# Order and size of the first weight transfers in a fused attention and SwiGLU layer

## The chip, the cores and the metric

The kernel runs on one core of one Trainium2 chip. The metric is device microseconds from launch to end, the median of several runs. A profiled execution is one more run, with its own time; its span is the time from its first to its last instruction.

## The reference

For x of 2048 rows (S) and 576 columns (D), bfloat16, with 32 heads of 18 columns, a window of 256 rows and F = 4608:

```python
xn = layernorm(x)
q, k, v = heads(xn @ wqkv)                      # 576 x 1728
scores  = q @ k.T * 18 ** -0.5                  # masked to 0 <= i - j < 256
attn    = softmax(scores) @ v @ wo
h       = silu(xn @ w1) * (xn @ w3)             # gate and up, 576 x 4608
out     = x + attn + h @ w2                     # 4608 x 576
```

## The kernel before, in words

**Engines and terms.** TensorE multiplies (PE in the profile), VectorE (DVE) and ScalarE (ACT) evacuate PSUM and do elementwise work, GpSimd (POOL) copies and masks, SyncE (SP) does nothing but issue DMA transfers. Every operation is recorded with `add(engine, function, r=reads, w=writes, j=joins)`. A key such as `"wv"` names a buffer; a reader waits for all writers of its keys, and an operation with `j` is one more writer of the same contents. `dma=` names the semaphore of a transfer. Each engine then executes its own operations strictly in the order in which they were recorded, so an instruction that waits holds up all that stands behind it on its engine.

**Tiling.** Rows come in four chunks of 512 (`NC`, `CH`), each of four tiles of 128 (`TB`). The 576 columns over which most products sum are held as five blocks, four of 128 and one of 64 that lies on both halves of the partitions. Matmuls with a contraction of 64 run in pairs, one on each half of the array.

**The start (from L730 on).**
1. The x tiles are loaded on SP's and ScalarE's queues. SP then loads V's weights: blocks 0 to 3 in one transfer (L733, key `wv`); block 4 comes on ScalarE's queue (key `wvd`).
2. SP loads q and k's weights into `wa`, a scratch area within the buffer `pt`: the first column half of q and of k (L753, key `wqk0`), the last 64 rows of all columns on both partition halves (L757, key `wqkd`), then the second column half (L753, key `wqk1`).
3. For each x tile: layer norm on VectorE and GpSimd, transposition on TensorE (`xn_turn`, L374), evacuation by ScalarE into `xnT` (L381). In between, the V projections of the first two tiles run on TensorE. At the second tile (`i == 1`) SP is given the six transfers of the first gate/up weight set (`load_w13`, L315), which wait for that tile's evacuation. A set holds 512 columns of w3 on partitions 0 to 63 and of w1 on partitions 64 to 127, in nine row blocks of 64.
4. `xn_swap` (L394): two transfers on SP copy `xnT` to `xnS` with the partition halves exchanged, since each gate/up product needs its input on both halves. They wait for all four tiles.
5. GpSimd deals q and k's weights from `wa` to `wp` in the order of heads that the attention wants (L807): four copies for the first half (key `wp0`), three for the second (`wp1`). The clearing of buffers and the masks stand behind them on GpSimd.
6. TensorE runs V for tiles 2 and 3 and the projections `("q", 0)` to `("q", 3)` and `("8", 7)` (L429). A projection has two parts, of five and four row blocks; the first part of the next stands between them. The pairs of output tiles are (0, 1), (2, 3), (8, 4), (5, 6) and 7; tiles over 3 need `wp1` as well. After `("q", 0)` SP gets four transfers of gate/up set 1 and the spreading of k's rows for the first two groups; after `("q", 2)` the rest of these, and set 1's last two transfers.

**The units.** A chunk then has 36 units (`unit_pairs`, L660) of nine matmul pairs: one for each 128 columns of gate and up, the first four pairs from `xnT`, the next four from `xnS`, the last from `xnT`. Units 0 to 3 use gate/up set 0, units 4 to 7 set 1. Between the pairs the planner places the attention's steps: scores (L553), their exponentials (L562) and masks (L589). It counts the pairs in `clock`, starts at `start` (28 in chunk 0, 42 in the others), and spreads the 32 steps of chunk 0 evenly over what is left, at least 7.5 apart. The value products (L610) follow 20 counts after a pair of groups is complete. Last come the products with w2 and wo (L711, L717).

Of the kernel before, what the change touches and what calls it, by code (L numbers as in the profile page):

```python
# [44 lines left out]
class _Prog:  # L45
# [13 lines left out]
    def add(self, eng, fn, r=(), w=(), j=(), dma=None, after=()):  # L59
        deps = []  # L60
        for k in r:
            deps += self.bufs[k].writers
        for k in w:
            g = self.bufs.get(k)
            if g is not None:
                deps += g.ahead(eng)
        for k in j:
            g = self.bufs[k].before
            if g is not None:
                deps += g.ahead(eng)  # L70
        op = _Op(eng, fn, deps + list(after), dma)
        op.after = tuple(after)
        self.n[eng] += 1
        op.pos = self.n[eng]
        if dma is not None:
            self.dma_count[dma] = self.dma_count.get(dma, 0) + 16
            op.cnt = self.dma_count[dma]
        for k in r:
            self.bufs[k].readers.append(op)
        for k in w:  # L80
            self.bufs[k] = _Gen([op], self.bufs.get(k))
        for k in j:
            self.bufs[k].writers.append(op)
        for k in w:
            if self.bufs[k].before is not None:
                self.bufs[k].before.before = None
        self.ops.append(op)
        return op
# [76 lines left out]
def bass_parallel_sum__sliding_block__glu_gated_swiglu__prompt_kernel(  # L165
# [11 lines left out]
    D = A_x.shape[2]  # L177
# [18 lines left out]
    add = P.add  # L196

    with ExitStack() as es:
# [14 lines left out]
        xnT = sb("xnT", [128, 2, 5, CH])  # L213
        xnS = sb("xnS", [128, 4, CH])
        wv = sb("wv", [128, 5, D])
        wp = sb("wp", [128, 5, 9, 128])
        wo = sb("wo", [128, 5, D])
        w13 = [sb(f"w13_{i}", [128, 9, 512]) for i in range(NW13)]
# [75 lines left out]
        nfill = 0  # L294

        def w13_at(k):
            if k == 3:
                return NW13, hT[:, 18:27, :]
            s = (k if k < 3 else k - 1) % NW13
            return s, w13[s]  # L300
# [3 lines left out]
        def load_part(after=(), behind=()):  # L304

            nonlocal nfill
            if nfill >= 6 * NC * NFC:
# [9 lines left out]
                src[192 * part:192 * part + 192, c0:c0 + 512].rearrange("(kd p) f -> p kd f", p=64)),  # L317
                r=list(behind), after=after, dma=f"w13_{s}_{n}", **{"j" if i else "w": [("w13", s)]})

        def load_w13(behind=(), parts=6):  # L320
            for _ in range(parts):
                load_part((), behind)
# [68 lines left out]
        def xn_swap(c, eng):  # L391
            for n in range(2):
                p, q = 64 * n, 64 - 64 * n
                add(eng[n], lambda e, p=p, q=q: e.dma_start(  # L394
                    xnS[p:p + 64, :, :], xnT[q:q + 64, c % 2, 0:4, :]),
                    r=xk(c), dma=f"xnS{n}", **{"j" if n else "w": ["xnS"]})

        def xk(c):
            return [("xnT", c % 2, tt) for tt in range(TB)]
# [6 lines left out]
        def proj_part(c, what, banks, part, behind=()):  # L406

            kind, i = what
            last = []
            for n in range(5 - part):  # L410
                for r in range(2):
                    x = r ^ part
                    kd, r0 = (4 if n == 4 else n), 64 * r
                    rows = slice(r0, r0 + 64)
                    out_ = PS[:, banks[x], :]
                    if kind == "q":
                        t = pair_of(c, i)[x]
                        st, mv = wp[rows, kd, t, :], xnT[rows, c % 2, kd, :]
                        keys = ["wp0"] + (["wp1"] if t > 3 else []) + xk(c)
                    elif kind == "8":  # L420
                        out_ = PS[:, banks[x], 0:CH // 2]
                        st, mv = wp[rows, kd, i, :], xnT[rows, c % 2, kd, x * (CH // 2):(x + 1) * (CH // 2)]
                        keys = ["wp0", "wp1"] + xk(c)
                    else:
                        out_ = PS[:, banks[x], 0:HD]
                        st, mv = xnT[rows, c % 2, kd, i * 128:(i + 1) * 128], wv[rows, kd, x * HD:(x + 1) * HD]
                        keys = ["wvd" if n == 4 else "wv", ("xnT", c % 2, i)]
                    first = part == 0 and n == 0
                    op = add("pe", lambda e, out_=out_, st=st, mv=mv, n=n, r0=r0, first=first: e.matmul(  # L429
                        out_, st, mv, start=first, stop=(part == 1 and n == 3), tile_position=(r0, 0)),  # L430
                        r=keys, after=behind if n == 0 else (), **{"w" if first else "j": [("ps", banks[x])]})
                    if n == 4:
                        last.append(op)
            return last
# [216 lines left out]
        def unit_pairs(c, u, n0, n1, b0):  # L651

            fc, fl = divmod(u, 4)
            sl, wt = w13_at(c * NFC + fc)
            for n in range(n0, n1):
                for r in range(2):
                    r0 = 64 * r
                    k = 8 if n == 8 else (2 * n + r if n < 4 else 2 * (n - 4) + 1 - r)
                    src = xnT[r0:r0 + 64, c % 2, k // 2, :] if n in (0, 1, 2, 3, 8) else xnS[r0:r0 + 64, n - 4, :]
                    op = add("pe", lambda e, n=n, r0=r0, r=r, k=k, src=src: e.matmul(  # L660
                        PS[:, b0 + r, :], wt[r0:r0 + 64, k, fl * 128:(fl + 1) * 128], src,
                        start=(n == 0), stop=(n == 8), tile_position=(r0, 0)),
                        r=[("w13", sl), "xnS"] + xk(c), **{"j" if n else "w": [("ps", b0 + r)]})
            return op

        def unit_tanh(u, b0):
# [63 lines left out]
        xslot = {}  # L730
        for t in range(TB):
            xslot[t] = load_x(t, "act" if t % 2 else "sp")
        add("sp", lambda e: e.dma_start(  # L733
            wv[:, 0:4, :], A_wqkv[0:512, 2 * D:3 * D].rearrange("(kd p) f -> p kd f", p=128)),
            w=["wv"], dma="wv")
        for p in range(2):
            add("act", lambda e, p=p: e.dma_start(
                wv[64 * p:64 * p + 64, 4, p * HD:(p + 1) * HD], A_wqkv[512:576, 2 * D + p * HD:2 * D + (p + 1) * HD]),
                dma="wvd", **{"j" if p else "w": ["wvd"]})
# [10 lines left out]
        for h in range(2):  # L750
            for n in range(2):
                c0 = n * D + h * HD
                add("sp", lambda e, c0=c0: e.dma_start(  # L753
                    wa[:, 0:4, c0:c0 + HD], A_wqkv[0:512, c0:c0 + HD].rearrange("(kd p) f -> p kd f", p=128)),
                    dma=f"wqk{h}", **{"j" if n else "w": [f"wqk{h}"]})
# [15 lines left out]
        moves = [], []  # L771
        for i in range(TB):
            if i + 1 < TB:
                for p in range(2):
                    ln_stats(i + 1, xslot[i + 1], p)
            ln_apply(i, xslot[i])
            if i == TB - 1:
                for move in moves[1]:
                    move()
            xn_turn(i, JOBS[1] if i % 2 else SC, "act")  # L780
            if i == 0:
                warm(3, 3)
            if i == 1:
                load_w13([("xnT", 0, 1)])
            proj_end(moves)
            if i < TB - 2:
                proj_begin(0, ("v", i))
        xn_swap(0, ("sp", "sp"))
        for move in moves[0]:
            move()  # L790
        for tt in (TB - 2, TB - 1):
# [3 lines left out]
        dealt = []  # L795
        for h in range(2):
            a, b = 4 * h, 4 * h + 4
            moves = [(wpf[:, :, a:b, 0:2 * Dh], wf[:, :, 0, a:b, :]),
                     (wpf[:, :, a:b, 2 * Dh:7 * Dh // 2], wf[:, :, 1, a:b, 0:3 * Dh // 2])]
            lo, hi = ((0, SPREAD), (SPREAD + 1, G))[h]  # L800
            s0 = lo - h
            moves.append((wpf[:, :, 8, s0 * Dh // 2:(s0 + hi - lo) * Dh // 2].rearrange("p k (g c) -> p k g c", c=Dh // 2),
                          wf[:, :, 1, lo:hi, 3 * Dh // 2:2 * Dh]))
            if h == 0:
                moves.append((wpf[:, :, :, 63], wf[:, :, 1, SPREAD, 3 * Dh // 2:2 * Dh]))
            for n, (dst, src) in enumerate(moves):
                dealt.append(add("pool", lambda e, dst=dst, src=src: e.tensor_copy(dst, src),  # L807
                                 r=[f"wqk{h}", "wqkd"], **{"j" if n else "w": [f"wp{h}"]}))
        for n in range(6):
            P.bufs[("pt", n)] = _Gen([], None)  # L810
            P.bufs[("pt", n)].readers = list(dealt)
# [10 lines left out]
        for what in [("q", 0), ("q", 1), ("q", 2), ("q", 3), ("8", 7), None]:  # L822
# [9 lines left out]
            if got and got[0] == "q" and got[1] < 3:  # L832
                for buf, key, rows in (((wo, "woz", (64, 4, 5)), (oT, "oTz", (64, 4, 5))),
                                       ((wo, "woz", (96, 0, 4)),), ((oT, "oTz", (96, 0, 4)),))[got[1]]:
                    r0, k0, k1 = rows
# [7 lines left out]
        for c in range(NC):  # L843
# [6 lines left out]
            total = 9 * NF + len(att) + 3 * PV_COST  # L850
            if c:
                total += 9 * sum(COST[kind] for kind, _ in PROJ)
            start = 28 if c == 0 else 42
            last = total - 24
            nxt = soon = start
            clock = 0.0
# [55 lines left out]
            for u in range(NF):  # L912
# [6 lines left out]
                b0 = jobs[u] = job()  # L919
# [11 lines left out]
                if next_pv in pv_ready and clock >= pv_ready[next_pv] and next_pv < 3:  # L931
                    j = next_pv
# [15 lines left out]
                if u in stat:  # L948
                    t = (c + 1) * TB + stat[u]
# [4 lines left out]
                if u in apply:  # L954
                    t = (c + 1) * TB + apply[u]
# [5 lines left out]
                if c == 0 and u == 13:  # L961
                    for t in range(4):
                        rows = A_wo[252 * (t // 2):252 * (t // 2) + 252, :].rearrange("(s p d) f -> p s d f", p=2, d=Dh)[t % 2, :, :, :]
                        add("sp", lambda e, t=t, rows=rows: e.dma_start(wo[0:126, t, :], rows),
                            r=["woz"], dma="wo", **{"j" if t else "w": ["wo"]})
# [14 lines left out]
            for n, item in enumerate(p2_list(c)):  # L980
# [20 lines left out]
                elif n in (100, 120) and c + 2 < NC:  # L1001
                    t = (c + 2) * TB + (n == 120)
# [32 lines left out]
```

## Time and profile before

| what | us |
|---|---|
| median of 3 runs | 563.96 |
| lowest and highest of these | 563.29, 564.82 |
| profiled execution | 562.66 |
| its span | 560.9 |
| TensorE busy in the span | 555.9 (99%) |
| first matmul with a q/k weight | 13.89 after the start |
| first gate/up matmul | 23.14 after the start |

The span is 1.76 us shorter than the profiled execution's own time; that rest lies before the first and after the last instruction. The granted clock of TensorE is 1.00 throughout.

In what follows, a timeline line gives the start and length in us, the engine and line, the operation, what it writes and reads, the count, and in brackets how long the engine was idle before it and what released it. A line of the windows gives a stretch of time, its length, then the busy time of TensorE, its weight loads, VectorE, ScalarE and GpSimd with the instruction counts, the granted clock, the share of time in which the DMA engines were busy, and GB/s. A line of waits gives who waited for whom, the total in us, how many times, and the longest.

### The profile page before, as it was taken

The numbers are of one execution on the slowest core, as the hardware profiler recorded it, in microseconds if no ns is written. First come the engines' busy times: TensorE is split into PE (matmuls) and PEld (weight loads), VectorE is DVE, ScalarE is ACT, GpSimd is POOL, SyncE is SP. The second block draws the span as 40 slices with busy tenths as digits, with TensorE's granted clock in tenths as the row PEclk, the third lists the DMA queues.
The fourth block names the chain that finished last, engine by engine and source line by source line (L and its number), as shares of the span: only waits on it lengthen the run. The fifth ranks groups of instructions, "written<-read, shape, count | busy, mean of one in ns | idle before, by whom it ended". The sixth has DMA issues, their size and how long they took to land.

```text
span 560.9 us, 15712 instructions
## 1 busy us (share of the span) xinstructions
PE 555.9 (99%) x6767; PEld 330.6 (59%) x6767; DVE 314.1 (56%) x586; ACT 254.8 (45%) x349; POOL 163.4 (29%) x384
## 2 busy tenths in 40 slices
PE   8999999999999999999999999999999999999998
PEld 4445554677655455477765555547776455455776
DVE  7567798710356778851046678884114577777211
ACT  4366666100287776600038777650005767765000
POOL 5533444300033445330003345423000343432000
DMA  9996969996466459578646644956862675351552
GB/s 227 236 174 157 205 161 187 169 237 186 127 137 139 113 138 168 132 154 234 181 101 139 158 123 108 183 154 151 209 180 68 138 171 133 91 142 54 138 148 64
DMA packets 126562, 85.75 MB, mean 153 GB/s; under 512 B 33973, under 2 KB 124269, under 8 KB 126493
## 3 DMA queue, kind: packets, MB, share of 16 engines
q1 hardware_dynamic: 124629, 82.69, 63.8%
q10 hardware_dynamic: 1864, 2.07, 1.3%
q8 instruction: 53, 0.87, 0.7%
q14 instruction: 16, 0.13, 0.1%
HBM read 71.22 MB, written 2.36 MB: 131 GB/s over the span
## 4 chain that ended last, share of the span: by engine, by line
PE 97%; DMA 1%; SPq 1%; POOL 0%; issue 0%; DVE 0%; POOLq 0%
PE ps L660 50%; PE ps L711 25%; PE ps L429 9%; PE ps L553 6%; PE ps L610 4%; PE ps L717 3%; DMA pt<-in_A_wqkv_dram 1%; POOL wp L807 0%; SPq L753 0%; SPq L291 0%; SPq L757 0%; DVE ofin L724 0%; SPq L733 0%; POOLq L154 0%
## 5 line engine op out<-in xcount | busy, mean ns | idle before, releaser
L660 PE MATMUL ps<-xnT,w 64*128 64x512 bf16 x1400 | 181.9, 376 | 0.0
L660 PE MATMUL ps<-xnS,w 64*128 64x512 bf16 x1120 | 149.7, 376 | 0.0
L711 PE MATMUL ps<-w,hT 128*128 128x288 bf16 x1152 | 146.4, 286 | 0.0
L675 DVE SCALAR_TENSOR_TENSOR gs<-th,ps 128x512 bf16<-128x512 bf16 x144 | 98.0, 681 | 79.5 <-ACT th L669 78.8
L562 ACT ACTIVATE pt<-ps 128x1024 bf16<-128x1024 f32 (+1 forms) x112 | 113.2, 1010 | 60.0 <-PE ps L553 59.7
L711 PEld LDWEIGHTS ps<-w,hT 128*128 128x128 bf16 x1152 | 112.3, 98 | 28.9 <-issue 0.2
L589 POOL TENSOR_TENSOR pt<-pt,mk 128x128 int32<-128x128 int32 (+1 forms) x199 | 80.7, 426 | 88.5 <-ACT pt L562 88.5
L678 DVE SCALAR_TENSOR_TENSOR hT<-gs,ps 128x512 bf16<-128x512 bf16 x144 | 98.9, 687 | 5.0
L660 PEld LDWEIGHTS ps<-xnT,w 64*128 64x128 bf16 x1400 | 65.1, 94 | 61.4 <-DVE hT L678 0.2
L669 ACT ACTIVATE th<-ps 128x512 bf16<-128x512 f32 x144 | 85.5, 593 | 31.3 <-PE ps L660 30.8
L660 PEld LDWEIGHTS ps<-xnS,w 64*128 64x128 bf16 x1120 | 53.3, 94 | 57.0
L724 DVE TENSOR_TENSOR ofin<-ps,xp 128x288 bf16<-128x288 f32 x32 | 14.7, 458 | 124.4 <-PE ps L717 124.4
L442 ACT ACTIVATE stage<-ps 128x512 bf16<-128x512 f32 x16 | 9.5, 596 | 143.3 <-PE ps L429 141.0
L589 POOL TENSOR_TENSOR hT<-hT,mk 128x128 int32<-128x128 int32 (+1 forms) x31 | 12.4, 421 | 161.8 <-ACT hT L562 161.8
L553 PE MATMUL ps<-qv,kv 64*128 64x320 bf16 (+4 forms) x528 | 51.3, 260 | 0.0
L553 PEld LDWEIGHTS ps<-qv,kv 64*128 64x128 bf16 x528 | 25.0, 94 | 28.3 <-ACT hT L562 1.9
L429 PE MATMUL ps<-xnT,wp 64*128 64x512 bf16 (+1 forms) x360 | 37.8, 355 | 0.5 <-POOL wp L807 0.5
L632 DVE STREAM_TRANSPOSE od<-oq 128x256 bf16<-128x256 bf16 x64 | 25.8, 427 | 6.3 <-POOL oq L625 6.3
L562 ACT ACTIVATE stage<-ps 128x1024 bf16<-128x1024 f32 x24 | 24.6, 1024 | 10.2 <-PE ps L553 10.0
L429 PEld LDWEIGHTS ps<-xnT,wp 64*128 64x128 bf16 x360 | 17.4, 94 | 16.9 <-POOL wp L807 0.8
L717 PE MATMUL ps<-wo,oT 128*128 128x288 bf16 x160 | 24.8, 286 | 0.0
L429 PE MATMUL ps<-wv,xnT 64*128 64x288 bf16 x288 | 22.2, 283 | 0.6 <-DMA wv<-in_A_wqkv_dram 0.3
(58 smaller groups left out, 332.6 us busy)
## 6 DMA issues: line engine op xcount, KB each, us to landing
w<-in_B_w_dram SPq DMA_DIRECT2D x210, 192.0 KB, 4.2
w<-in_B_w_dram SPq DMA_DIRECT2D x72, 288.0 KB, 3.5
xp<-in_A_x_dram SPq DMA_DIRECT2D x28, 144.0 KB, 4.1
out_dram<-ofin SPq DMA_DIRECT2D x32, 72.0 KB, 3.2
xnS<-xnT SPq DMA_DIRECT2D x8, 256.0 KB, 4.8
oT<-od SPq DMA_DIRECT2D x48, 36.0 KB
pt<-in_A_wqkv_dram SPq DMA_DIRECT2D x4, 288.0 KB, 7.5
hT<-in_B_w_dram SPq DMA_DIRECT2D x6, 192.0 KB, 3.9
```

The costliest lines, as they stand in the source:

```text
L429: op = add("pe", lambda e, out_=out_, st=st, mv=mv, n=n, r0=r0, first=first: e.matmul(out_, st, mv, start=first, stop=(part == 1 and n == ...
L553: add("pe", lambda e, r0=r0, out_=out_, kb=kb, q0=q0, nb=nb: e.matmul(out_, kb4[r0:r0 + 64, g, kb + NV - NB, :] if kb < 0 else kv[r0:r0 + ...
L562: add("act", lambda e: e.activation(pt_slot(sl)[:, 0:w, :], PS[:, SC[0]:SC[1] + 1, 0:w].rearrange("p r q -> p q r"), ACT.Exp, scale=scale) ...
L589: add("pool", lambda e, vb=vb, mm=mm: e.tensor_tensor(vb, vb, mm, ALU.mult), r=(key if n == 0 else []) + ["mk"], **{"w" if n == 0 else "j" ...
L610: add("pe", lambda e, p=p, q=q, pr=pr, sl=sl, g=g, pos=pos, q0=q0, nb=nb, col=col, first=first, n=n: e.matmul(PS[32 * q:32 * q + VW, banks ...
L632: add("dve", lambda e: e.transpose(od[i][:, g % 2, c0:c0 + CH // 2], oq[:, c0:c0 + CH // 2]), r=["oq", "oq0"], **{"j" if half or g % 2 els ...
L660: op = add("pe", lambda e, n=n, r0=r0, r=r, k=k, src=src: e.matmul(PS[:, b0 + r, :], wt[r0:r0 + 64, k, fl * 128:(fl + 1) * 128], src, star ...
L669: add("act", lambda e: e.activation(th[i][:], PS[:, bg, :], ACT.Tanh, scale=0.5), r=[("ps", bg)], w=[("th", i)])
L675: add("dve", lambda e: e.scalar_tensor_tensor(out=gs[i][:], in0=th[i][:], scalar=1.0, in1=PS[:, bg, :], op0=ALU.add, op1=ALU.mult), r=[("t ...
L678: add("dve", lambda e: e.scalar_tensor_tensor(out=hT[:, u, :], in0=gs[i][:], scalar=0.5, in1=PS[:, bu, :], op0=ALU.mult, op1=ALU.mult), r= ...
L711: add("pe", lambda e: e.matmul(bank, hT[:, f, tt * 128:(tt + 1) * 128], w2[sl][:, k, :], start=(f == 0), stop=False), r=[("h", f), ("w2", ...
L717: add("pe", lambda e: e.matmul(bank, oT[:, k, tt * 128:(tt + 1) * 128], wo[:, k, d0:d0 + HD], start=False, stop=(k == 4)), r=[("oT", j) fo ...
```

## The change

- V's weights, blocks 0 to 3, come in two transfers of two blocks each (keys `wv0`, `wv1`). Each pair of V's matmuls waits for the transfer that holds its block.
- The first half of q and k's weights is dealt in eight copies in place of four: four for blocks 0 to 3, which wait for `wqk0` alone and write `wp0`, then four for block 4, which wait for `wqkd` and write a new key `wpr`. Only matmuls with block 4 (and those of tile 7, all of them) read `wpr`.
- Gate/up set 0 comes in two column halves of 256, each of two transfers with all nine row blocks. The first half (key `w13_first`) takes the place of the six transfers; the swap of the input follows it; then comes the second half. Units 0 and 1 of chunk 0 wait for the first half, units 2 and 3 for the second.
- The planner's `start` for chunk 0 goes from 28 to 32.

```diff
+        def load_first(half, behind=()):
+            nonlocal nfill
+            nfill = 6
+            s, dst = w13_at(0)
+            c0 = 256 * half
+            for n in range(2):
+                src = (B_w3, B_w1)[n]
+                add("sp", lambda e, n=n, src=src: e.dma_start(
+                    dst[64 * n:64 * n + 64, :, c0:c0 + 256],
+                    src[:, c0:c0 + 256].rearrange("(kd p) f -> p kd f", p=64)),
+                    r=list(behind), dma=f"w13_{s}_{n}" if half else f"w13_first_{n}",
+                    **{"j" if n else "w": [("w13", s) if half else "w13_first"]})
...
-                        keys = ["wp0"] + (["wp1"] if t > 3 else []) + xk(c)
+                        keys = ["wpr" if n == 4 else "wp0"] + (["wp1"] if t > 3 else []) + xk(c)
...
-                        keys = ["wp0", "wp1"] + xk(c)
+                        keys = ["wpr", "wp0", "wp1"] + xk(c)
...
-                        keys = ["wvd" if n == 4 else "wv", ("xnT", c % 2, i)]
+                        keys = ["wvd" if n == 4 else f"wv{n // 2}", ("xnT", c % 2, i)]
...
-                        r=[("w13", sl), "xnS"] + xk(c), **{"j" if n else "w": [("ps", b0 + r)]})
+                        r=["w13_first" if c == 0 and u < 2 else ("w13", sl), "xnS"] + xk(c),
+                        **{"j" if n else "w": [("ps", b0 + r)]})
...
-        add("sp", lambda e: e.dma_start(
-            wv[:, 0:4, :], A_wqkv[0:512, 2 * D:3 * D].rearrange("(kd p) f -> p kd f", p=128)),
-            w=["wv"], dma="wv")
+        for n in range(2):
+            add("sp", lambda e, n=n: e.dma_start(
+                wv[:, 2 * n:2 * n + 2, :], A_wqkv[256 * n:256 * n + 256, 2 * D:3 * D].rearrange("(kd p) f -> p kd f", p=128)),
+                w=[f"wv{n}"], dma=f"wv{n}")
...
             if i == 1:
-                load_w13([("xnT", 0, 1)])
+                load_first(0, [("xnT", 0, 1)])
...
         xn_swap(0, ("sp", "sp"))
+        load_first(1)
...
-            for n, (dst, src) in enumerate(moves):
-                dealt.append(add("pool", lambda e, dst=dst, src=src: e.tensor_copy(dst, src),
-                                 r=[f"wqk{h}", "wqkd"], **{"j" if n else "w": [f"wp{h}"]}))
+            for k0, k1, need, key in ((0, 4, ["wqk0"], "wp0"), (4, 5, ["wqkd"], "wpr")) if h == 0 else ((0, 5, ["wqk1", "wqkd"], "wp1"),):
+                for n, (dst, src) in enumerate(moves):
+                    dealt.append(add("pool", lambda e, dst=dst[:, k0:k1], src=src[:, k0:k1]: e.tensor_copy(dst, src),
+                                     r=need, **{"j" if n else "w": [key]}))
...
-            start = 28 if c == 0 else 42
+            start = 32 if c == 0 else 42
```

## The prediction

> **What bounds the kernel now.** I read the page first: the busy shares and the 40 slices.
>
> ```profile
> span 560.9 us, 15712 instructions
> ...
> PE 555.9 (99%) x6767; PEld 330.6 (59%) x6767; DVE 314.1 (56%) x586; ACT 254.8 (45%) x349; POOL 163.4 (29%) x384
> ...
> PE   8999999999999999999999999999999999999998
> ```
>
> TensorE is busy in every slice but the two ends, so 5.0 us of the span is idle there. The windows say where the ends are.
>
> ```profile
> 0.00:5.00 5.00, 3.75 (x9) 1.34 (x10) 3.42 (x7) 1.28 (x1) 3.13 (x11) 1.00 0.62 174
> 5.00:10.00 5.00, 4.46 (x51) 2.06 (x51) 4.27 (x15) 1.41 (x2) 3.08 (x7) 1.00 1.08 276
> 10.00:15.00 5.00, 4.47 (x76) 2.74 (x74) 3.20 (x8) 3.71 (x8) 2.33 (x5) 1.00 1.11 244
> 15.00:20.00 5.00, 5.00 (x52) 2.42 (x50) 2.59 (x6) 1.40 (x3) 4.66 (x9) 1.00 1.05 277
> ...
> 558.00:560.90 2.90, 0.20 (x2) 0.00 (x0) 0.46 (x1) 0.00 (x0) 0.00 (x0) 1.00 0.16 51
> ```
>
> The columns are time, TensorE's busy time, then the other engines', the granted clock (1.00 throughout) and the DMA share. Idle are 1.25 us before the first matmul, 0.54 and 0.53 us in the next two stretches, and 2.70 us at the end. The change touches neither the first nor the last. That leaves 1.07 us, and TensorE's own list of waits names it:
>
> ```profile
> PE ps L745 <- DVE oq L740: 1.2, 1, 1.2
> PE ps L429 <- POOL wp L807: 0.5, 1, 0.5
> PE ps L429 <- DMA wv<-in_A_wqkv_dram: 0.3, 1, 0.3
> PE ps L429 <- ACT xnT L381: 0.2, 1, 0.2
> ```
>
> Limited to 14 to 540 us that list is empty but for the 0.5 us at 13.9, so the rest is one unbroken stream of a fixed number of matmuls. Last the timeline of the stretch in question, and the chain of waits:
>
> ```profile
> 7.96 0.79 PE L429 MATMUL ps<-wv,xnT 64*128 64x288 bf16 x10 [0.33 <-DMA wv<-in_A_wqkv_dram]
> 9.66 4.35 SPq L315 DMA_DIRECT2D w<-in_B_w_dram  x6
> 11.43 2.00 PE L429 MATMUL ps<-wv,xnT 64*128 64x288 bf16 x28
> 12.03 1.80 POOL L807 COPY wp<-pt 128x720 f32<-128x720 f32 x4 [2.26 <-DMA pt<-in_A_wqkv_dram]
> 13.89 1.25 PE L429 MATMUL ps<-xnT,wp 64*128 64x512 bf16 x10 [0.46 <-POOL wp L807]
> 14.06 1.25 SPq L394 DMA_DIRECT2D xnS<-xnT  x2
> 14.48 1.65 POOL L807 COPY wp<-pt 128x720 f32<-128x720 f32 x3 [0.64 <-DMA pt<-in_A_wqkv_dram]
> ```
>
> ```profile
> 3.92 7.97 DMA pt<-in_A_wqkv_dram
> ...
> 12.03 1.81 POOL wp L807 x4
> ...
> 13.89 9.41 PE ps L429 x98
> ```
>
> The chain: q and k's weights land, POOL deals them out, the first q/k projection starts at 13.89, and from there TensorE never stops. Whatever moves the start of that projection moves the end of the kernel, at most by the idle time above.
>
> **The change part by part.**
>
> *Dealing split by rows.* The four first copies waited for both first column blocks (wqk0) and the last 64 rows (wqkd). Issue plus landing time puts wqk0's two transfers at 2.18 + 6.3 = 8.5 and 2.73 + 8.0 = 10.7 us, wqkd's at 3.28 + 6.8 = 10.1 and 3.92 + 8.0 = 11.9. Now four copies of four row blocks wait for 10.7 alone, and four of the fifth block for 11.9. Lengths: copies of 720, 540 and 45 elements took 787, 637 and 258 ns, so about 0.83 ns an element on 0.19 us. Four fifths of each of 720, 540, 135 and 45 give 0.67 + 0.55 + 0.28 + 0.25 = 1.75 us. The old four add up so to 1.99 where the timeline shows 1.80, so I take 0.19 off: 1.56. POOL is free at 9.77 (its last layer-norm step starts at 9.20 and takes 0.57), so the first set is dealt at 10.75 + 1.56 = 12.3. The fifth block's copies (144, 108, 27, 9 elements) take 1.06 - 0.19 = 0.87 and end at 13.2. The extra POOL time is 0.6 us, which lies in the wait for wqk1 that ended at 14.48; without that cover it would delay the second half's dealing by as much. The mask and clearing work queued behind on POOL keeps its place.
>
> TensorE reached the first q projection after the V part's 28 matmuls, at 13.43, and stood 0.46 us. The dealt weights are now there by 12.3, so the 0.46 us goes, and still would if V ended 0.3 us earlier. What comes late next is the fifth block, needed four pairs into the projection: 0.85 us after its start of 13.15 (below), 14.0, against 13.2. After it come the second half's weights, dealt at 14.48 + 1.65 = 16.13 and wanted by the third projection, which started near 17.4 and will want them near 16.65.
>
> *V's weights in two transfers.* The whole landed at 1.71 + 6.2 = 7.91, and TensorE waited 0.33 us. The first tile's transposed input is ready at 6.92 + 0.70 = 7.62, so V cannot start before 7.68 (0.06 from evacuation to matmul, as at 9.63 to 9.69): at most 0.28 us. Its first two pairs need the first transfer, the next two the second. Bytes ahead of it on the queue are the same, so I leave the second's landing at 7.91. At 0.16 us a pair it is wanted at 8.00: no wait. The gain survives to 13.43 because each later step waits for its predecessor: the third tile's normalised input is ready at 9.25 and its transposes start at 10.32, the fourth's at 10.44 and 11.04. Both leave more than 0.28. Bounds: +0.28, if the first half is early and the second not late. At the other end the second transfer lands 0.45 us late, the price of one more issue (SP's V issue took 0.43): V then ends about 0.1 later than before. I take 0.28: V's packets run until 7.4 us, well after both issues, so the queue and not the issue sets the landing.
>
> What speaks against dividing a transfer is that each has a part that its bytes don't explain (an x tile of 144 KB took 2.8 us to land on an empty queue). Paid one after the other, it would turn this edit round (third rival). But the six weight transfers issued 0.72 us apart from 9.66 on landed 4.8 to 5.2 us after issue each, so about 0.8 us apart: that part overlaps. The Trainium skill, "DMA: Bandwidth & Descriptors", section Anatomy of one DMA, fits a transfer on GpSimd's path as 2.0 us fixed plus its bytes; read as serial, it would give V's second half at 9.9 and a sum of 1.2 us lost instead of 0.74 gained, and the spacing just shown doesn't bear that reading out for SP's queue.
>
> The additional issue also moves the q/k weight issues 0.45 us back. DMA share is 0.62 up to 5 us and 1.08 after, with 7 to 8.7 us from issue to landing, so I price it at nothing, with 0.45 us on all q/k landings as the other end: dealt at 12.75 (hidden), fifth block 13.65 (hidden), second half 16.6 against 16.65 wanted. Even that end costs at most about 0.1.
>
> *First gate/up set in column halves, swap between.* SP issued six transfers for 4.35 us from 9.66, then the swap at 14.06. Now two at 9.38 (the same tile's evacuation, 0.28 earlier), done near 10.8, the swap as soon as the last input tile is evacuated (12.10 - 0.28 = 11.82), two more by 14.4, then the four of set 1, which so start 0.9 us earlier than 15.35. None of this waits for anything new, except that the second half and all behind it queue on SP behind the swap's wait, some 1 us in which SP would otherwise be free. Units 0 and 1 need half the columns. But the first unit did not wait before, so this gains nothing; it only gives room for a start 0.74 us earlier. The cost is lines of 512 bytes for 1,024: 2,304 packets for 1,152. In the trace's packet records a 576-byte packet took 32 ns on average before 8 us and 46 after, a 1,024-byte one 69 and 65. At 46 the half takes 1,152 x 46 / 16 = 3.3 us against 2.3 for the same bytes before. Chaining from the last q/k landing, 14.4: first half 17.7, swap (1.8) 19.5, second half 22.8. They are wanted at 22.3 (23.04 - 0.74), 23.2 and 26.2. Covered, by 3.4 us at the least.
>
> *Start 28 to 32.* With the plan's arithmetic worked through for both values, the first six attention steps of chunk 0 stand 2 to 6 matmul pairs later (at 0.216 us), and the seventh to the last in the same places, as do all value products. Same matmuls: zero. The keys of the first groups were in by 26 us (128-byte packets end there) and the first step moves from 29.19 to about 29.3.
>
> **Sum.** 0.46 + 0.28 = 0.74 us off. The profiled execution took 562.66 (span 560.9 and 1.76 around it), 1.30 under the median of the runs, so 561.92 in a profile (span 560.2) and 563.96 - 0.74 = 563.2 as median. That is 0.13%, below the 0.3% (1.7 us) that a measurement here can tell from no change.
>
> **The rivals.**
>
> 1. *Part of the gain is lost on the way*, because V's second half or the second dealing comes late: 0.1 to 0.5 us gained, 563.5 to 563.9. For it: margins of 0.1 to 0.8 us in what is late next. Against: the saturated queue. Chance 0.26.
> 2. *Slower: the narrower lines or divided transfers set the queue back.* Place: the SP queue up to the keys of the first groups and set 1. At 68 ns per 512-byte packet, as much as a line of twice the size took, each half takes 4.9 us. The second half then lands at 26.0, level with its need. The next four transfers (0.78 each) land at 29.1 and the first keys near 30, 0.8 us after the first attention step wants them. Set 1's rest would come near 31.5 for unit 4's 30.3: some 1.2 to 2 us of standing, net 0.5 to 1.3 slower, 564.5 to 565.2. It decides from about 60 ns on; each further 10 ns adds 1.4 us, so over 0.3% slower needs some 75. Against: the 46 ns. Chance 0.11.
> 3. *Slower: transfers on one queue pay their fixed part in turn.* V's second half then lands up to 2.8 us late, at 10.7 for a need at 8.0; V ends near 15.9 in place of 13.15, q/k start there, 2.0 us later than before: 566.0. Against: landings 0.8 us apart. Chance 0.03.
> 4. *More than forecast*: a gain over 1.1 us. The 1.07 us of idle is a cap, save 0.3 us hidden in the 28 matmuls (2.00 us where 14 pairs at 0.12 take 1.68) and the spread of the runs, 563.29 to 564.82. Chance 0.07.
>
> The forecast itself has 0.53. The range takes the forecast, rival 1 and the lower part of rival 2, with half a microsecond for the median of a few runs: 562.2 to 564.7. Over 0.3% either way needs more than the named idle time, or the far end of rival 2 or rival 3: 0.09 and 0.10, with 0.81 between.
>
> **What would show it.** In the changed profile the first copy on POOL starts near 10.8, V near 7.7, the q projection at 13.1 to 13.2 with no wait on POOL, the swap on SP near 11.9, the first gate/up matmul at 22.3, and no wait of TensorE after that. A q/k start at 13.4 to 13.6 means rival 1; a wait of a gate/up or score matmul on a DMA between 22 and 32 us, rival 2. A span change with the gate/up start unchanged would show the whole reading wrong.

## The result, and the profile after

The changed kernel is slower: 565.69 us (median of 15) against 563.62 for the kernel before beside it, ratio 1.0043 with a 95% interval of 1.0023 to 1.0063. The prediction had 563.2 and a range to 564.7. The start of the kernel went almost as forecast. Eight microseconds after the first gate/up matmul, at a place that the forecast had not followed to its end, TensorE stands.

The first lines are from the page of the changed kernel (lines of the code lie 14 to 18 further on: L443 was L429, L674 was L660, L825 was L807). The row PEclk is the granted clock of TensorE in tenths; the page of the kernel before has no such row.

```profile
span 565.8 us, 15715 instructions
...
PE 556.8 (98%) x6767; PEld 336.3 (59%) x6767; DVE 313.9 (55%) x586; ACT 255.3 (45%) x349; POOL 164.3 (29%) x388
...
PEclk9989999999999999999999999999999999999999
```

TensorE's list of waits, changed kernel:

```profile
PE ps L674 <- issue: 2.6, 1, 2.6
PE ps L388 <- DVE xn L376: 1.4, 1, 1.4
PE ps L761 <- DVE oq L756: 1.2, 1, 1.2
PE ps L732 <- issue: 0.3, 1, 0.3
PE ps L726 <- DMA w<-in_B_w_dram: 0.3, 1, 0.3
PE ps L443 <- ACT xnT L395: 0.2, 1, 0.2
```

The waits for dealt weights (0.5 us) and for V's weights (0.3) are gone. The 1.4 us ahead of the transposes (L388) are not work lost: x landed 0.4 us later in this execution, and the warm-up matmuls ended 1.2 us earlier. New are one wait of 2.6 us at a gate/up matmul and two of 0.3 us late in the kernel (L726, L732). The word "issue" stands for a wait whose releaser the profile does not name. The timeline shows the two ends of the story:

```profile
10.75 2.29 POOL L825 COPY wp<-pt 128x576 f32<-128x576 f32 x8 [0.61 <-DMA pt<-in_A_wqkv_dram]
12.09 1.17 SPq L408 DMA_DIRECT2D xnS<-xnT  x2
13.23 1.24 PE L443 MATMUL ps<-xnT,wp 64*128 64x512 bf16 x10
14.26 1.65 POOL L825 COPY wp<-pt 128x720 f32<-128x720 f32 x3 [1.21 <-DMA pt<-in_A_wqkv_dram]
...
33.33 1.04 PE L674 MATMUL ps<-xnT,w 64*128 64x512 bf16 x8 [2.57 <-issue]
```

The first q projection starts at 13.23 (13.15 forecast, 13.89 before), with no wait on GpSimd. The first gate/up matmul starts at 22.50 (23.14 before). At 33.33 begins unit 4, which is the first to read gate/up set 1. A transfer leaves 16 steps of its semaphore in the trace, and the last of them is its landing. The last step of set 1's last transfer comes at 33.24; before it came at 29.24, when unit 4 started at 31.35 (within the last of these lines of the chain before) and waited for nothing:

```profile
29.57 1.51 PE ps L660 x14
31.08 0.22 PE ps L553 x6
31.30 1.94 PE ps L660 x18
```

The chain of waits of the changed kernel then shows a second loss behind the first:

```profile
29.89 0.86 PE ps L674 x8
30.76 2.57 issue
33.33 1.25 PE ps L674 x10
34.58 0.25 PE ps L567 x6
34.83 3.38 PE ps L674 x16
38.21 0.19 PE ps L567 x4
38.40 1.73 PE ps L674 x16
```

Sixteen matmuls take 3.38 us at 34.83 and 1.73 at 38.40. The windows say why; the third number from the end is the granted clock:

```profile
30.00:33.30 3.30, 0.76 (x8) 0.20 (x4) 2.11 (x4) 1.44 (x2) 0.73 (x2) 1.00 1.12 210
33.30:34.80 1.50, 1.48 (x18) 0.93 (x20) 0.00 (x0) 0.00 (x0) 0.00 (x0) 0.95 1.14 244
34.80:38.20 3.40, 3.40 (x21) 1.44 (x18) 0.96 (x2) 1.62 (x2) 0.87 (x2) 0.52 0.86 186
38.20:40.00 1.80, 1.80 (x23) 0.96 (x20) 0.41 (x1) 1.40 (x2) 0.56 (x2) 1.00 0.60 88
```

So this execution (567.53 us) lost 2.57 us standing, 1.65 us at half the clock, and 0.6 us in two later waits, and won 0.64 at the start: 4.2 of the 4.9 us by which it is longer than the profiled one of before. The other 0.7 us are not accounted for. A mean granted clock below 1.00 goes with the long executions: of the 15, ten had 1.000 and took 564.2 to 566.1 us, five had 0.994 to 0.997 and took 567.5 to 569.4.

### The profile page after: what moved, and what is told of

Read it like the earlier page. It is cut to its first block, busy times and chain, and to the rows that moved or that the text cites. A ratio compares the mean times of both kernels' runs of the same rounds, so it can differ in the third digit from the quotient of the medians.

```text
span 565.8 us, 15715 instructions
## 1 busy us (share of the span) xinstructions
PE 556.8 (98%) x6767; PEld 336.3 (59%) x6767; DVE 313.9 (55%) x586; ACT 255.3 (45%) x349; POOL 164.3 (29%) x388
## 4 chain that ended last, share of the span: by engine, by line
PE 96%; DMA 2%; issue 1%; DVE 0%; ACT 0%; POOL 0%; SPq 0%
PE ps L674 50%; PE ps L726 24%; PE ps L443 9%; PE ps L567 6%; PE ps L624 3%; PE ps L732 3%; DMA w<-in_B_w_dram 1%; DMA xp<-in_A_x_dram 1%; ACT xnT L395 0%; PE ps L388 0%; DVE xn L376 0%; SPq L741 0%; POOL rstd L370 0%; DVE stats L364 0%; DVE ofin L739 0%
## 5 line engine op out<-in xcount | busy, mean ns | idle before, releaser
L674 PE MATMUL ps<-xnT,w 64*128 64x512 bf16 x1400 | 184.3, 378 | 2.6 <-issue 2.6
L674 PE MATMUL ps<-xnS,w 64*128 64x512 bf16 x1120 | 151.4, 377 | 0.0
L726 PE MATMUL ps<-w,hT 128*128 128x288 bf16 x1152 | 146.6, 286 | 0.3 <-DMA w<-in_B_w_dram 0.3
L726 PEld LDWEIGHTS ps<-w,hT 128*128 128x128 bf16 x1152 | 112.3, 98 | 29.3 <-DMA w<-in_B_w_dram 0.6
L674 PEld LDWEIGHTS ps<-xnT,w 64*128 64x128 bf16 x1400 | 68.2, 94 | 63.2 <-issue 4.5
L684 ACT ACTIVATE th<-ps 128x512 bf16<-128x512 f32 x144 | 85.5, 594 | 33.1 <-PE ps L674 32.6
L674 PEld LDWEIGHTS ps<-xnS,w 64*128 64x128 bf16 x1120 | 55.5, 94 | 54.3 <-issue 0.2
L443 PE MATMUL ps<-xnT,wp 64*128 64x512 bf16 (+1 forms) x360 | 38.0, 355 | 0.0
L576 ACT ACTIVATE stage<-ps 128x1024 bf16<-128x1024 f32 x24 | 24.6, 1024 | 10.3 <-PE ps L567 10.1
L443 PEld LDWEIGHTS ps<-xnT,wp 64*128 64x128 bf16 x360 | 17.7, 94 | 16.1 <-issue 0.7
L732 PE MATMUL ps<-wo,oT 128*128 128x288 bf16 x160 | 24.8, 286 | 0.3 <-issue 0.3
L443 PE MATMUL ps<-wv,xnT 64*128 64x288 bf16 x288 | 22.2, 283 | 0.4 <-ACT xnT L395 0.2
```

Of the source, the lines that this page charges most:

```text
L576: add("act", lambda e: e.activation(pt_slot(sl)[:, 0:w, :], PS[:, SC[0]:SC[1] + 1, 0:w].rearrange("p r q -> p q r"), ACT.Exp, scale=scale) ...
L684: add("act", lambda e: e.activation(th[i][:], PS[:, bg, :], ACT.Tanh, scale=0.5), r=[("ps", bg)], w=[("th", i)])
L726: add("pe", lambda e: e.matmul(bank, hT[:, f, tt * 128:(tt + 1) * 128], w2[sl][:, k, :], start=(f == 0), stop=False), r=[("h", f), ("w2", ...
L732: add("pe", lambda e: e.matmul(bank, oT[:, k, tt * 128:(tt + 1) * 128], wo[:, k, d0:d0 + HD], start=False, stop=(k == 4)), r=[("oT", j) fo ...
```

## The experiments

What was in question: theory A says that the 512-byte lines put SP's queue back until set 1 is late; B that the order does it, with the swap between the halves; C that the transfers land as ever and TensorE merely comes earlier. Each kernel stood beside the kernel before on its chip, and medians are given as "this / before". The ratio behind them comes from all executions of both, with a 95% interval, and is not quite the quotient of the medians. The diffs show the lines that make the edit; the keys that the readers wait for change with them.

### The parts of the gate/up edit

**Row lines.** The changed kernel without the column halves.

```diff
-                load_first(0, [("xnT", 0, 1)])
+                load_w13([("xnT", 0, 1)])
...
-        load_first(1)
```

> The changed kernel with gate/up set 0 as before: six transfers by rows with 1,024-byte lines ahead of the swap; V's two transfers, the divided dealing and start 32 stay. Theory A (512-byte lines put SP's queue back by some 1.6 us, and set 1's last two transfers land after TensorE reaches unit 4): no wait at unit 4, set 1's last transfer lands near 29 us, q/k start at 13.2, time 562.7 to 563.2 where the kernel before gives 563.6. Theory C (TensorE merely arrives 0.74 us earlier than transfers that land as before): a wait of 0.5 us or more at unit 4 and a time within 0.2 us of the kernel before.

Measured: 563.21 / 563.93 us, ratio 0.9992 (0.9977 to 1.0007). The chain of waits runs through unit 4's start, at 30.64, without a stop:

```profile
29.94 1.94 PE ps L674 x18
31.88 0.22 PE ps L567 x6
32.10 1.73 PE ps L674 x16
```

Set 1's last transfer landed at 30.2, 1.2 us after the forecast and 0.4 us ahead of unit 4. The missing wait speaks against C; the time is not told apart from before.

**Columns only.** The kernel before with the halves and start 32, V and the dealing as before.

```diff
-                load_w13([("xnT", 0, 1)])
+                load_first(0, [("xnT", 0, 1)])
...
         xn_swap(0, ("sp", "sp"))
+        load_first(1)
...
-            start = 28 if c == 0 else 42
+            start = 32 if c == 0 else 42
```

> The kernel before with only set 0's column halves, the swap between them, and start 32; V and the dealing as before. Theory A: q/k start at 13.9, set 1's last transfer lands near 33 us, TensorE waits 1.3 to 2 us at unit 4 (wanted near 31.5), time 565.0 to 567 with the granted clock sometimes under 1. Theory C: no wait at unit 4, time as before, 563.6.

Measured: 565.99 / 563.93, ratio 1.0038 (1.0017 to 1.0059). TensorE comes later here than before (first gate/up at 23.64) and still waits:

```profile
30.93 0.86 PE ps L674 x8
31.79 2.50 issue
34.29 1.25 PE ps L674 x10
```

The last step of set 1 is at 34.20. This edit alone costs as much as the whole change, and C falls. The clock stayed at 1.00 in this profile, after a wait of 2.50 us.

**Order and line size apart.** First 1,024-byte lines in the new order, then 512-byte lines in the old one.

```diff
-                load_first(0, [("xnT", 0, 1)])
+                load_w13([("xnT", 0, 1)], 3)
...
-        load_first(1)
+        load_w13((), 3)
```

> The changed kernel with 1,024-byte lines in the changed order: three row transfers, the swap, three row transfers (every unit waits for all six). Theory A (line size): like the run with row lines ahead of the swap, no wait at unit 4, 562.7 to 563.2. Theory B (the order, with SP standing at the swap before it issues the rest, is what puts the queue back): a wait of about 2 us at unit 4 as in the changed kernel, 565 or more.

Measured: 563.93 / 563.93, ratio 1.0010 (0.9987 to 1.0032), with a wait of 1.2 us in the profile. That lies between the two theories: 0.7 us over the row lines with the swap at the end.

```diff
                 load_first(0, [("xnT", 0, 1)])
+                load_first(1)
...
-        load_first(1)
```

> The changed kernel with both column halves issued ahead of the swap: 512-byte lines in the order of before. With row lines, the swap in the middle measured 0.72 us more than the swap at the end (563.93 against 563.21). Line size as main cause: a wait of 1 us or more at unit 4 remains, set 1's last transfer lands after 31.5 us, 564.5 to 566. Order as main cause: no wait at unit 4, 563.0 to 563.5.

Measured: 565.41 / 563.72, ratio 1.0026 (1.0002 to 1.0051), a wait of 1.7 us, the last step of set 1 at 32.10, and four of twelve executions with a granted clock under 0.998. Against the row lines in the same order (563.21, on another chip) that is 2.2 us. The column halves are the larger part; the order adds less, and with this spread its 0.7 us is not firm. The halves are also four transfers in place of six, which no run separates from the line size.

### What makes the lag a wait

Between the two first profiles the lag is 1.6 us when set 0 and the swap are in (21.96 against 20.35) and 1.7 when set 1's first four transfers are (25.0 against 23.27), but 4.0 us for the last. Set 0's packets account for the 1.6: their times in the trace's packet records, summed and divided by the 16 DMA engines, come to 4.7 us before (1,152 packets of 1,024 bytes) and 6.3 after (2,304 of 512). Something else meets set 1's last two transfers. ScalarE issues q's spread for groups 2 to 7 beside them, first in the kernel before, then in the changed one:

```profile
23.99 2.02 SPq L315 DMA_DIRECT2D w<-in_B_w_dram  x3
24.87 1.52 ACTq L494 DMA_DIRECT2D qv<-stage  x2
...
23.31 2.74 SPq L315 DMA_DIRECT2D w<-in_B_w_dram  x2
24.20 1.84 ACTq L508 DMA_DIRECT2D qv<-stage  x2
```

Its packets are of 6,144 bytes and took 0.49 us each in the packet records of the changed kernel. By 27.0, 322 of set 1's last 384 packets and 4 of q's 72 had started in the kernel before; in the changed kernel 174 and 9.

**Set 1 ahead of the keys.**

```diff
-                load_w13((), 4)
+                load_w13((), 6)
...
-                load_w13((), 2)
```

> The changed kernel with all six transfers of gate/up set 1 issued after the first q projection, so that its last two no longer stand behind the last keys of the first groups. If the wait at unit 4 is one for set 1's last two transfers (theory A), it is gone: these land by 27 us. What comes late next are the first groups' keys, some 1.6 us later, near 28 to 30 us, wanted at 29.4: a wait of 0 to 1 us at the first score step; time 562.8 to 564. If the wait at unit 4 is for something else, it stays near 2.5 us and the time near 565.5.

Measured, in seven executions: 567.98 / 563.93, ratio 1.0055 (1.0022 to 1.0088). The wait at unit 4 is gone, and the first score step waits for the keys instead:

```profile
25.88 6.64 DMA kv<-stage
32.52 0.05 issue
32.57 0.39 PE ps L567 x4
```

So the wait at unit 4 was for set 1. But I had the next wait at 0 to 1 us, and it is 3.1: the keys' last transfer landed at 32.5, not 28 to 30. What stands last in this stretch pays, whichever it is.

**q's late transfers moved.** The two q transfers are issued at unit 3, near 31 us; their readers come at 43.

```diff
-        span_main(2, G, "act", slice(0, 2))
...
-                    span_main(2, G, "act", slice(2, None))
+                    span_main(2, G, "act")
```

> The changed kernel with the two 216 KB transfers that spread q's rows of groups 2 to 7 (6,144-byte packets, ScalarE's queue, issued near 24.2 us) moved to unit 3, near 30 us; nobody reads them before 43 us. Theory Q (their packets share the DMA engines with set 1's last two transfers and turn a lag of 1.6 us into one of 4): set 1's last transfer lands near 31, the wait at unit 4 falls from 2.6 to 0 to 1 us, 563 to 564.3. If only the backlog on SP's own queue counts: wait and time stay, 565 to 566.

Measured, with the column halves as they are: 563.17 / 563.72, ratio 0.9994 (0.9977 to 1.0012). Set 1's first four transfers are in at 24.97, as late as in the changed kernel, but its last step comes at 30.1, and unit 4 starts without a stop:

```profile
30.14 1.94 PE ps L674 x18
32.08 0.22 PE ps L567 x6
32.30 1.73 PE ps L674 x16
```

Set 1's last 384 packets started between 25.4 and 27.9 here, between 25.4 and 30.1 in the changed kernel. This is the strongest evidence that q's packets hold set 1 up: not one byte or line of SP's transfers was changed.

The same move in the row lines kernel:

```diff
-                load_first(0, [("xnT", 0, 1)])
+                load_w13([("xnT", 0, 1)])
...
-        load_first(1)
...
-        span_main(2, G, "act", slice(0, 2))
...
-                    span_main(2, G, "act", slice(2, None))
+                    span_main(2, G, "act")
```

> The row-line kernel (V's two transfers, divided dealing, set 0 by rows ahead of the swap, start 32) with the same q transfers moved to unit 3. Theory Q: set 1's last transfer lands near 28.5, some 2 us before it is wanted, and the time loses its runs above 563.9: median 562.6 to 563.1. Otherwise 563.2 as without the move.

Measured, with row lines: 562.91 / 563.72, ratio 0.9979 (0.9963 to 0.9996), set 1 in at 28.0, all twelve executions between 562.31 and 563.33. This beats both kernels.

And in the kernel before, where it is the whole edit:

```diff
-        span_main(2, G, "act", slice(0, 2))
...
-                    span_main(2, G, "act", slice(2, None))
+                    span_main(2, G, "act")
```

> The kernel before with only q's two transfers for groups 2 to 7 moved to unit 3. If the kernel before too sometimes waits for set 1 (its times reach 567 in a few executions): the profile looks the same, the times above 564.5 vanish, and the median falls by 0.2 to 0.5 us to 563.2 to 563.5. If the gain of the row-line kernel with this move comes from the start alone: as before, 563.7.

Measured, the kernel before with this move alone: 562.92 / 563.72, ratio 0.9982 (0.9968 to 0.9997), none over 563.91. The median fell by 0.8 us, more than the 0.2 to 0.5 expected. That fits a kernel before that waits for set 1 too in some of its executions, but no profile of it caught such a wait, and when this kernel was measured again (below) it had one execution at 565.19.

The profiles of all runs show how the two delays meet. The last step of set 1 came at (left out are the two kernels with another order of set 0 by rows or of set 1):

| set 0 | q's late transfers in place | moved to unit 3 |
|---|---|---|
| by rows | 29.2, 29.7, 30.2, 30.8, 33.1 | 27.7, 28.0, 28.4, 28.6 |
| in column halves | 32.1, 33.1, 33.2, 34.2 | 30.1, 30.7 |

By the means, q's transfers cost 2.4 us with rows and 2.8 with halves, and the halves 2.6 and 2.2 us. As far as this scatter tells, the two delays add. The 4.0 us above come from setting the changed kernel against the earliest landing in this table's first cell; that the lag grows among q's packets is not shown.

### The clock

The changed kernel with twelve matmuls on zeros ahead of unit 4:

```diff
                 b0 = jobs[u] = job()
+                if c == 0 and u == 4:
+                    warm(b0[0], 12)
```

> The changed kernel with 12 matmuls on zeros ahead of unit 4, 2.6 us in which TensorE otherwise stands; their results are overwritten. Theory H (the executions of 567.5 to 569.4 us are those in which the standing TensorE is given half its clock for 1.7 or 3.4 us): no granted clock under 0.999, no time over 566.5, median 564.7 to 565.5. If the low clock has nothing to do with the wait: a third of the times stay at 567 to 569.

Measured: 566.53 / 563.72, ratio 1.0045 (1.0028 to 1.0062); granted clock 1.000 in all twelve, where the changed kernel had five of fifteen below. Theory H holds for the clock. On the time I missed: half the executions were over 566.5, up to 568.45. The filling costs its full 2.6 us where the wait is shorter: 562.9 without a wait plus 2.6 is 565.5, the lowest time seen. What is above it may be waits longer than the filling; only one execution has a profile, and it shows none.

### The parts of the start

Three edits, each put alone into the kernel before. **The dealing:**

```diff
-                        keys = ["wp0"] + (["wp1"] if t > 3 else []) + xk(c)
+                        keys = ["wpr" if n == 4 else "wp0"] + (["wp1"] if t > 3 else []) + xk(c)
...
-            for n, (dst, src) in enumerate(moves):
...
+            for k0, k1, need, key in ((0, 4, ["wqk0"], "wp0"), (4, 5, ["wqkd"], "wpr")) if h == 0 else ((0, 5, ["wqk1", "wqkd"], "wp1"),):
...
```

> The kernel before with only the dealing divided by rows (V in one transfer, set 0 by rows ahead of the swap, start 28). By the prediction's sum: q/k start at 13.4 to 13.5 instead of 13.9, no wait of TensorE on GpSimd, 0.46 us gained, near 563.2 where before gives 563.7. If the dealing was not what held TensorE: no gain.

Measured: 563.58 / 563.72, ratio 1.0000 (0.9985 to 1.0014): the 0.46 us expected do not show. The q projection starts at 13.27, even before the expected 13.4, with no wait on GpSimd. But the profiled execution waits 2.3 us at unit 4 with 1,024-byte lines as well; the chain from 28 us on:

```profile
24.62 7.77 DMA w<-in_B_w_dram
32.38 0.77 issue
33.15 1.90 PE ps L674 x16
```

In this execution ScalarE issued q's first transfer at 24.23, ahead of both of set 1's last (24.62 and 25.32); in the profile of before it came behind both.

**V:**

```diff
-        add("sp", lambda e: e.dma_start(
-            wv[:, 0:4, :], A_wqkv[0:512, 2 * D:3 * D].rearrange("(kd p) f -> p kd f", p=128)),
-            w=["wv"], dma="wv")
+        for n in range(2):
+            add("sp", lambda e, n=n: e.dma_start(
+                wv[:, 2 * n:2 * n + 2, :], A_wqkv[256 * n:256 * n + 256, 2 * D:3 * D].rearrange("(kd p) f -> p kd f", p=128)),
+                w=[f"wv{n}"], dma=f"wv{n}")
```

> The kernel before with only V's weights in two transfers. V starts at 7.7 instead of 7.96, but the dealing, which ended last, still waits for the last 64 rows, whose issue SP makes 0.45 us later: q/k start between 13.9 and 14.4, gain 0, loss up to 0.5 us: 563.7 to 564.2. If V was what held the start: 0.28 gained, 563.4.

Measured: 563.37 / 563.72, ratio 0.9994 (0.9982 to 1.0005). I expected nothing, since the undivided dealing came last. In its profile V starts at 7.46 and the q projection at 12.77, because the last 64 rows of q and k's weights landed at 10.05, not the 11.9 of before.

**The hand number of the order:**

```diff
-            start = 28 if c == 0 else 42
+            start = 32 if c == 0 else 42
```

> The kernel before with only the planner's start at 32. By the prediction no change: within 0.2 us of before. If the place of the first attention steps matters by itself: 0.5 us or more either way.

Measured: 563.90 / 563.72, ratio 1.0011 (0.9996 to 1.0025): no change that can be told, as forecast.

**Does the gain arrive?** Three kernels on one chip, all the kernel before with q's late transfers moved: with the V and dealing diffs above added, with nothing added, and with the columns-only diff added.

> The kernel before with q's late transfers moved to unit 3, V in two transfers and the divided dealing (set 0 by rows, start 28). Beside the same kernel without V's and the dealing's edits, on the same chip: if the 0.74 us of the forecast reach the end once set 1 is not late, it is 0.4 to 0.8 us faster (562.2 to 562.5 if that one gives 562.9). If an earlier start is given back at another wait: within 0.2 us of it.

> The kernel before with only q's late transfers moved to unit 3, as measured once at 562.9: the measure for the two others on this chip. 562.7 to 563.1.

> The same with set 0 in column halves, the swap between them, and start 32 (V and the dealing as before). If the column halves cost only through set 1's late landing among q's transfers: within 0.3 us of the kernel with the move alone. If 512-byte lines cost by themselves: 1 us or more slower, with a wait at unit 4.

Measured, beside 563.66 for before: 563.01 with the start's edits (0.9988, 0.9977 to 0.9999), 563.10 without (0.9993, 0.9978 to 1.0007), 564.01 with the column halves (1.0002, 0.9988 to 1.0017). In the profiles the first gate/up matmul comes 0.86 us earlier with the edits (22.06 against 22.92) and the span ends 0.7 earlier (560.4 against 561.1), but the medians differ by 0.09, which is the outcome named for a gain that is given back. In these two profiles the lead is still 0.8 us at 508 us, so no later wait takes it back. It is a favourable pair, though: over all profiles the first gate/up matmul came at 22.5 on average in the nine kernels with both edits of the start (22.06 to 22.84) and at 23.0 in the four with neither and set 0 by rows (22.92 to 23.14). The halves have no wait at unit 4 in their profile, but one of 0.5 us at a later gate/up matmul and one of 0.5 at w2's weights. So moving q's transfers takes away most of their loss, perhaps not all: 0.9 us between medians whose intervals overlap, where 0.3 was expected, and 0.3 between the two kernels with the start's edits (563.17 and 562.91).

## Why the prediction was wrong

**Right.** What bounds the kernel, and what the start would do: the dealing by rows took away the 0.46 us, the fifth block and the second half were ready in time, and the first gate/up matmul came 0.64 us earlier for 0.74 forecast. V's share was smaller than its 0.28: it started at 7.92 (7.68 forecast, 7.96 before) in this execution, where x came late, and on average at 7.7 in the ten profiles with two V transfers against 7.9 in the seven with one. 512-byte packets took 41 ns on average up to 15 us and 46 after (46 was assumed). Set 0's halves and the swap landed at 17.2, 19.0 and 21.96, each ahead of the 17.7, 19.5 and 22.8 that the prediction chained. `start` cost nothing that can be told.

**The step that failed** is "Covered, by 3.4 us at the least". That margin is of set 0's second half. The lag does not end there: SP's queue hands it on to all that stands behind, and set 1's last step came at 33.24, while TensorE stood before unit 4 from 30.76 on, for 2.57 us. The numbers were in the trace of before: it came at 29.24 for a start of unit 4 at 31.35, 2.1 us of cover. The earlier start would take 0.74 of it, and by the forecast's own 3.3 us for 2.3 the two halves 2.0. That is 0.6 us short; with the 1.7 us measured it is 0.3. Rival 2 named this place ("Set 1's rest would come near 31.5 for unit 4's 30.3", where 31.35 less 0.74 gives 30.6), but bound it to 68 ns a packet and had it decide "from about 60 ns on". It decided at 41 to 46. Its 1.2 to 2 us of standing are near the 2.57 measured, but for another reason than the one it gave, so that nearness is luck.

**The term that was missing** is ScalarE's queue. Rival 2's chain added the lengths of SP's transfers as if they had the DMA engines to themselves: at 46 ns in place of 68 it puts set 1's rest at 28.3 (31.5 - 3.2), and without the halves' 2.0 us at 26.3, where the trace of before has 29.24. q's 6,144-byte packets cost 2.4 to 2.8 us there, with rows as with halves. With them moved, the same halves caused no stop at unit 4.

**The clock** was taken as 1.00 throughout, since the trace of before shows nothing else. A stand of 2.57 us was followed by 3.4 us at 0.52 of it. The Trainium skill, "TensorE: Matmul & The Clock Gate", section What's actually happening, describes a gate that halves the clock after an idle window of about 3.4 us, and says that the window runs freely. The length of the slow stretch agrees: in the clock records it runs from 34.64 to 38.06, 3.41 us. So does its place: full clock had been granted at 3.92, nine such lengths before. The idle time that sufficed here, 2.57 us, was shorter than the page's window; the measurement decides. The 3.1 us wait with set 1 ahead of the keys was followed by 3.41 us at half clock as well, while 2.50 us (columns only) and 2.3 us (deal only) left it at 1.00.

**The chances**: 0.11 for rival 2 and 0.10 for over 0.3% slower were too low, in hindsight, for a change that lengthens the busiest queue where the DMA share is over 1.

**Open.** Whether the gain at the start reaches the end: one pair of profiles says 0.7 us, the medians 0.1. And in the traces some steps of a transfer come 1 to 3 us after the others (in the changed kernel 13 of the 16 steps of set 0's third transfer by 18.81, the last at 20.39). That decides when a transfer has landed, and the experiments do not say what makes those steps late.

## What to carry to other kernels

Follow a queue's lag to the last transfer behind it, and compare each with its own need; the one nearest to its need, not the one edited, sets the price. Add to a landing time what other queues have in flight at that moment: moving a transfer that nobody wants yet took 0.8 us off the median in one measurement and 0.6 in another (the second within its interval), the work at the start 0.1 more. Compare several profiles before reading a difference of a microsecond in a landing: the kernel before and deal only, with the same transfers, differed by 3.8 us in the landing of set 1. A wait of TensorE of some 2.6 us can cost 1.65 us more in clock, so a mean granted clock under 1.00 points to a stand.

## What the runs showed of the hardware

- With one 576 KB transfer divided in two, what stands behind it mostly landed earlier, though it was issued half a microsecond later: q and k's first weights were in at 8.77 to 10.70 us in the ten profiles with two V transfers (nine of them by 10.28) and at 10.28 to 11.19 in the seven with one. No run shows why.
- A packet of half the size took about two thirds of the time: 41 to 46 ns for 512 bytes in the changed kernel, 65 to 69 for 1,024 in the same stretches of the trace before.
- Half clock came in a stretch of 3.41 us, in the profiles after waits of 2.57 and 3.1 us and not after 2.50 or 2.3, and twelve matmuls on zeros ahead of unit 4 kept it away in twelve executions.
